# A chunked scan with two MLPs on one core: Silu by ScalarE in two blocks, and C B^T from rounded parts in the last twelve units

## The chip, the cores and the metric

One core of a Trainium2 chip runs the whole program. The metric is the device time of one execution in microseconds (us); lower is better. The core has five engines with a queue of instructions each, worked off in order: TensorE (PE, with its weight loads PEld), VectorE (DVE), ScalarE (ACT), GpSimd (POOL) and SyncE (SP, which here issues every DMA). A semaphore ties an instruction to what it needs on another engine.

## What is computed

The reference is a chain of three parts, all in float32:

```python
# 1: scan over 24 chunks of 32 steps, 4 batches x 8 heads, head_dim 32, state 16
M = einsum('bhin,bhjn->bhij', Cc, Bc) * L          # L = exp(cum_i - cum_j), lower triangle
y = M @ xc + (Cc @ state) * exp(cum)
state = exp(sum la) * state + Bx.sum
# 2: x = y as [3072, 256]
xn = x / sqrt(mean(x*x) + 1e-6) * rms_g
g = xn @ w_gate;  val = xn @ w_val                 # 256 -> 1536
x2 = (g * sigmoid(g) * val) @ w_out                # 1536 -> 256
# 3: h = x2 @ w_in (256 -> 1024); solu = h * softmax(h); layer norm over 1024, times g_ln
out = ln @ w_out2                                  # 1024 -> 256
```

## The kernel before, in words

The kernel uses chunks of 128 steps, not 32. A *unit* is 128 tokens of one batch with all 8 heads; there are 24 units (6 per batch, which carry a state from one to the next), in six *blocks* of 4 units, 512 tokens each.

**A unit's attention step.** `at_cb` (line 290) multiplies C by B^T for the eight heads, contraction over 16 rows, in float32: 8 matmuls, which the profile shows as 16 records. `at_mt` (L307, DVE) multiplies the result by the decay L, which ACT made with an exponential (`at_lexp`, L237; in the first four units `at_lpx`, L267). `at_y` (L321, L326, L331) makes the rows and the state's part; `at_ycb` issues the next unit's `at_cb` right behind it. Then follow a square (`at_sq`, L355, ACT), its column sum (`at_ms`, L361, PE), the root (L374, L379), its broadcast (L383), the copy and scale (`at_xc` L389, `at_xn` L394) and the split into a rounded part and a remainder (`at_xh` L401, `at_xl` L405).

**The split.** The large products run on operands that are rounded (fp32r), each as a rounded part and a remainder: high by high, low by high, high by low. So a 256-deep gate product of 512 tokens is 6 matmuls.

**The first MLP of a block** goes in 12 slices f of 128 of the 1536 features: gate (`pg`, L558), value (`pv`, L558), `th` = tanh(g/2) on ACT (L572), (th+1) g on DVE (`g_silu`, L576), times the value on DVE (`g_mul`, L580), rounding to `ah` (ACT, L586), remainder `al` (DVE, L592), and 2 x 3 matmuls into `po` (L600). `pg` and `pv` have one PSUM bank each, so the next gate product waits until the last one was read. The factor 2 that this form leaves is taken out at `x2_h` and `x2_l` (scale 0.5).

**The second MLP of a unit**: `ph` (L436, 12 matmuls), maximum, exponential, product on DVE and ACT, transposes `pt` (L514), split, `pf` (L538, 24 matmuls), output.

**Weights** arrive as raw 64-bit words. A piece (26 of them, 512 KB each) takes three DVE passes (`w_conv`: L116, L119, L122), a rounding on ACT (`w_hi`, L129) and a remainder on DVE or POOL (`w_lo`, L133). This work lies in the first 140 us, beside the start and the first blocks' MLP.

**The order** is written by a planner at build time. Each step is an `op` with an engine, an assumed duration, a due time, the steps it follows, the buffers it makes and uses. `plan` (in the same function) takes, again and again, the engine that can start first, and on it the step with the earliest due time among those that could start within a small slack; some DVE steps have an alternative on POOL (`alt`). Due times come from constants: `PRO` and `FIRST` (when block 0's MLP is due and how long it lasts), `Y0`, `YPOS` (attention steps), `EARLY`, `WGAP` (weights), `HLAG` (second MLP). What comes out is a fixed order on each engine.

Of the kernel before, what the change touches and what calls it, by code (L numbers as in the profile page):

```python
# [7 lines left out]
F32 = mybir.dt.float32  # L8
# [4 lines left out]
ALU = mybir.AluOpType  # L13
# [29 lines left out]
WGAP = 8.0  # L43
HLAG = (50.0, 26.0)
# [7 lines left out]
def fused_kernel(ctx, tc, aT, xbt, bcT, wg, wv, wo1, rg, wi2, wo2, gl, consts, out):  # L52
# [333 lines left out]
    def at_xc(u):  # L386
        d = st[u]
        d["xts"] = sp.tile([P, 2, P], F32, name="xts", bufs=BUFS["xts"])
        A.activation(d["xts"], d["y"][:, 0:256].rearrange("p (g i) -> p g i", g=2), AF.Copy)  # L389

    def at_xn(u):
        d = st[u]
        for g in range(2):
            V.scalar_tensor_tensor(out=d["xts"][:, g], in0=d["xts"][:, g], scalar=rgt[:, g:g + 1],  # L394
                                   in1=d["y"][:, 384:512], op0=ALU.mult, op1=ALU.mult)
# [293 lines left out]
    for u in range(NU):  # L689
# [7 lines left out]
        op(f"lbc{u}", "SP", 0.85, Y - 9, (ld_bc, u), new=[("bc", f"bc{u}")], kb=128)  # L697
# [32 lines left out]
        cbop = f"cb{u}" if u <= blk[0][1] else f"y{u-1}"  # L730
# [3 lines left out]
        yc = blk[0][1] <= u < NU - 1  # L734
# [17 lines left out]
        op(f"xc{u}", "ACT", 0.42, Y, (at_xc, u), after=[f"y{u}", f"sq{u}"], new=[("xts", f"xt{u}")], use=[f"y{u}", f"xt{u}"])  # L752
        op(f"xn{u}", "DVE", 0.6, Y, (at_xn, u), after=[f"rb{u}", f"xc{u}"], use=[f"y{u}", f"xt{u}"])
# [6 lines left out]
    for b in range(NB):  # L760
# [3 lines left out]
        for f in range(NF):  # L764
# [11 lines left out]
            op(f"si{s}", "DVE", v_us(N), t, (g_silu, b, f), after=[f"th{s}"], use=[f"th{s}", f"pg{s}"])  # L776
            op(f"mu{s}", "DVE", v_us(N), t, (g_mul, b, f), after=[f"si{s}", f"vm{s}"], use=[f"th{s}", f"pv{s}"])
# [123 lines left out]
    op("wd", "ACT", 0.35, 5.5, (c_wdec,), after=["sf"], use=["pd"])  # L901
    op("cst", "SP", 0.9, 5, (ld_cst,), kb=128)
    op("glt", "SP", 0.45, 40, (ld_glt,), kb=4)
    for u in range(2):
        ops[f"sbd{u}"]["after"].append("cst")
        ops[f"xn{u}"]["after"].append("cst")
# [3 lines left out]

    def plan():
        users = {}
        for o in ops.values():
            for key in set(o["use"]):
                users[key] = users.get(key, 0) + 1
# [25 lines left out]
        def est(o, e, margin=0.0):  # L941
            t = free[e]
            for a in o["after"]:
# [12 lines left out]
            if e == "SP" and len(dma_end) >= 8:  # L956
                t = max(t, dma_end[-8])
            return t

        while len(order) < len(ops):  # L960
            best = None
            dve = None
            for e, names in ready.items():
                if e == "POOL":
                    names = names + [nm for nm in ready["DVE"] if "alt" in ops[nm] and nm != dve]
                c = [(est(ops[nm], e, MARGIN.get(e, 0.0) if free[e] > PRO else 0.0), nm) for nm in names]
# [14 lines left out]
            if e != o["e"]:  # L981
                o = ops[nm] = dict(o, us=o["alt"][0], fn=o["alt"][1])
                ready["DVE"].remove(nm)
            else:
                ready[e].remove(nm)
            order.append((t, nm))
            if e == "SP":
                free[e] = t + o["us"]
                dma_free = max(dma_free, t + 1.3) + o["kb"] / 300.0
# [21 lines left out]
    with tc.manual_schedule():  # L1011
        S.dma_start(la, aT)
        S.dma_start(um, consts[:, 0:3 * P])
        S.dma_start(ident, consts[:, 3 * P:4 * P])
# [14 lines left out]
        V.tensor_scalar(out=nid, in0=ident, scalar1=-1.0, scalar2=None, op0=ALU.mult)  # L1029
# [70 lines left out]
```

## Time and profile before

| | us |
|---|---|
| median of 3 runs (565.73 to 566.2) | 565.83 |
| the profiled execution | 565.08 |
| its span, first to last instruction | 563.4 |
| PE busy | 546.5 (97%) |
| DVE busy | 390.9 (69%) |
| ACT busy | 290.3 (52%) |
| POOL busy | 84.8 (15%) |

The profiled execution is one of its own; its time lies 0.75 us under the median. "Busy" for PE means that at least one matmul was in flight; matmuls overlap, so a group's busy time is larger than what it adds to the path. The pitch from one start to the next is the better measure of cost. PEclk is the granted TensorE clock as a share of full speed; 0.50 is its lower level.

### The profile page before, as it was taken

Reading aid. Unit: us, or ns where it says so; the run is one execution under the profiler, and the core shown is the slowest. Engines: PE = TensorE matmul, PEld = TensorE weight load, DVE = VectorE, ACT = ScalarE, POOL = GpSimd, SP = SyncE. Lnnn points to the kernel's source line nnn. Section 1 sums busy time; section 2 is a strip of 40 time slices with the busy share of each in tenths; the row PEclk is TensorE's granted clock in tenths of the full one; section 3 lists DMA queues with packets and bytes.
Section 4 is the critical chain, followed back from the end, with each engine's and each line's share of the span. In section 5 each row is a group of like instructions: output and inputs, shape, how many; then the busy total and the mean of one; then the engine's idle time right before and its main releaser. Section 6 shows DMA issues by size and latency. Waiting matters only on the chain.

```text
span 563.4 us, 9443 instructions
## 1 busy us (share of the span) xinstructions
PE 546.5 (97%) x3544; PEld 461.1 (82%) x3544; DVE 390.9 (69%) x789; ACT 290.3 (52%) x654; POOL 84.8 (15%) x118
## 2 busy tenths in 40 slices
PE   9879998899999999999999999999999999999996
PEld 8757886687888888888888888888888888888795
DVE  5788999999876776575684574684674574564763
ACT  6437654666555564463474454554543353343464
POOL 2333323212221010110111100110100000000010
PEclk9579999999999999999999999999999999999999
DMA  7464765542022021121120220220200000000000
GB/s 213 132 212 140 216 203 194 182 145 71 14 72 76 2 80 47 43 72 36 54 76 11 75 70 10 80 70 10 72 2 9 10 1 9 11 1 10 9 20 30
DMA packets 44366, 39.33 MB, mean 70 GB/s; under 512 B 3936, under 2 KB 36896, under 8 KB 44320
## 3 DMA queue, kind: packets, MB, share of 16 engines
q1 hardware_dynamic: 44320, 38.72, 22.5%
q8 instruction: 28, 0.46, 0.4%
q14 instruction: 18, 0.15, 0.1%
HBM read 35.37 MB, written 3.34 MB: 69 GB/s over the span
## 4 chain that ended last, share of the span: by engine, by line
PE 81%; DVE 15%; DMA 2%; issue 1%; ACT 1%; SPq 0%; POOL 0%; DVEq 0%; ACTq 0%; POOLq 0%
PE pv L558 15%; PE pg L558 15%; PE po L600 14%; PE ph L436 12%; PE pf L538 12%; PE pt L514 4%; PE pcb L301 3%; DVE wt L119 2%; PE y L326 2%; DVE wt L122 2%; DVE th L580 2%; PE y L321 1%; DVE al L592 1%; DVE th L576 1%; DVE L L307 1%; DVE wt L116 1%
## 5 line engine op out<-in xcount | busy, mean ns | idle before, releaser
L586 ACT ACTIVATE ah<-th 128x512 fp32r<-128x512 f32 x72 | 45.2, 628 | 52.2 <-PE po L600 38.8
L580 DVE TENSOR_TENSOR th<-pv,th 128x512 f32<-128x512 f32 x72 | 49.8, 691 | 29.2 <-PE pv L558 24.1
L592 DVE TENSOR_TENSOR al<-th,ah 128x512 fp32r<-128x512 f32 x70 | 49.3, 704 | 26.0 <-ACT ah L586 25.6
L576 DVE SCALAR_TENSOR_TENSOR th<-th,pg 128x512 f32<-128x512 f32 x72 | 49.1, 682 | 20.0 <-ACT th L572 19.7
L558 PE MATMUL pg<-xh,wg_h 128*128 128x512 f32 x144 | 59.5, 413 | 2.3 <-ACT xh L401 1.2
L600 PE MATMUL po<-ah,wo_h 128*128 128x512 f32 x144 | 60.3, 419 | 0.0
L600 PE MATMUL po<-al,wo_h 128*128 128x512 f32 x144 | 56.7, 394 | 2.3 <-DVE al L592 2.3
L558 PE MATMUL pv<-xh,wv_h 128*128 128x512 f32 x144 | 58.4, 406 | 0.0
L558 PE MATMUL pg<-xh,wg_l 128*128 128x512 f32 x144 | 57.0, 396 | 0.0
L558 PE MATMUL pg<-xl,wg_h 128*128 128x512 f32 x144 | 56.8, 394 | 0.0
L600 PE MATMUL po<-ah,wo_l 128*128 128x512 f32 x144 | 56.7, 394 | 0.0
L558 PE MATMUL pv<-xl,wv_h 128*128 128x512 f32 x144 | 56.5, 392 | 0.0
L558 PE MATMUL pv<-xh,wv_l 128*128 128x512 f32 x144 | 56.4, 392 | 0.0
L572 ACT ACTIVATE th<-pg 128x512 f32<-128x512 f32 x72 | 42.6, 592 | 26.6 <-PE pg L558 26.4
L502 POOL TENSOR_TENSOR sc<-sc,mhalf 128x1 f32<-128x1 f32 x24 | 14.1, 587 | 263.6 <-DVE sc L497 263.6
L237 ACT ACTIVATE L<-L,cneg 128x128 f32<-128x128 f32 x160 | 50.5, 390 | 0.6 <-DMA L<-crow 0.6
L460 ACT ACTIVATE ut<-ph,sc 128x1024 f32<-128x1024 f32 x20 | 22.3, 1116 | 54.5 <-DVE sc L447 54.5
L538 PE MATMUL pf<-wo_h,uth 128*128 128x256 f32 x176 | 49.6, 282 | 0.3 <-DVE utl L528 0.2
L538 PE MATMUL pf<-wo_h,utl 128*128 128x256 f32 x176 | 49.6, 282 | 0.0
L538 PE MATMUL pf<-wo_l,uth 128*128 128x256 f32 x176 | 49.5, 281 | 0.0
L447 DVE TENSOR_REDUCE sc<-ph 128x1 f32<-128x1024 f32 x20 | 24.5, 1225 | 31.7 <-PE ph L436 31.7
L523 ACT ACTIVATE uth<-pt 128x512 fp32r<-128x512 f32 x44 | 26.0, 595 | 31.1 <-PE pt L514 30.9
(138 smaller groups left out, 1225.2 us busy)
## 6 DMA issues: line engine op xcount, KB each, us to landing
L<-crow SPq DMA_DIRECT2D x20, 512.0 KB
stage<-in_wo_dram SPq DMA_DIRECT2D x10, 512.0 KB
xb<-in_xbt_dram SPq DMA_DIRECT2D x24, 192.0 KB
stage<-in_wg_dram SPq DMA_DIRECT2D x6, 512.0 KB
bc<-in_bcT_dram SPq DMA_DIRECT2D x48, 64.0 KB
stage<-in_wv_dram SPq DMA_DIRECT2D x6, 512.0 KB
out_dram<-ob SPq DMA_DIRECT2D x24, 128.0 KB
stage<-in_wi_dram SPq DMA_DIRECT2D x4, 512.0 KB
```

Source lines behind the costliest of these rows:

```text
L237: A.activation(d["L"][:, h], d["L"][:, h], AF.Exp, bias=cneg[:, u * 8 + h:u * 8 + h + 1])
L436: T.matmul(ph[c], xx[:, kk, k * P:(k + 1) * P], ww[:, kk, 512 * c:512 * c + 512], start=(i == 0), stop=(i == 5))
L447: V.tensor_reduce(out=sc[:, 0:1], in_=ph[0], axis=AX.X, op=ALU.max, negate=True)
L523: A.activation(d["uT"][0][:, 4 * c:4 * c + 4].rearrange("p k t -> p (k t)"), d["ptc", c], AF.Copy)
L538: T.matmul(d["pf"][:, 0:DM], uu[:, k], ww[:, k], start=(k == 0 and i == 0), stop=(k == 7 and i == 2))
L558: T.matmul(ps[:, :n], ww[:, kk, f * P:(f + 1) * P], xx[:, kk, :n], start=(i == 0), stop=(i == 5))
L572: A.activation(d["th"], d["pg"], AF.Tanh, scale=0.5)
L576: V.scalar_tensor_tensor(out=d["th"], in0=d["th"], scalar=1.0, in1=d["pg"], op0=ALU.add, op1=ALU.mult)
L580: V.tensor_tensor(out=d["th"], in0=d["pv"], in1=d["th"], op=ALU.mult)
L586: A.activation(d["ah"], d["th"], AF.Copy)
L592: e.tensor_tensor(out=d["al"], in0=d["th"], in1=d["ah"].bitcast(F32), op=ALU.subtract)
L600: T.matmul(po[b, m][:, :n], ww[:, f, m * P:(m + 1) * P], aa, start=(f == 0 and i == 0), stop=(f == NF - 1 and i == 2))
```

## The change

1. In blocks 0 and 1 ACT computes Silu(g) itself; the DVE step `g_silu` is gone there and the product becomes (2 silu) times value. Silu lies in another activation table than the exponential, so the built program has more table loads on ACT.
2. For units 12 to 23, B and C come by one DMA into 128 rows: the same 32 rows four times (512 KB written instead of 128). ACT rounds both (`at_hi`); DVE or POOL puts the remainder of B into the lower 64 rows (`at_blo`), DVE the remainder of C by a mask in rows of odd slots (`at_clo`); two masked copies separate the two heads that share 32 rows (`at_c0` on ACT, `at_c1` on DVE). One matmul of 128 rows and 256 columns then adds all four products of parts for two heads: 4 matmuls a unit. They are a step of their own and no longer tied to `at_y`.
3. The row scale `rms_g` moves from DVE (`at_xn`, two passes, now one) to ACT (`at_xc`, one pass, now two).
4. Where the planner sees PE idle for over 0.5 us during the start, it puts in small matmuls on unused columns (`warm`); five stand in the program. The identity's load is a planned step, and its negative is no longer made.
5. Constants of the planner change, and it counts 1.3 us for a change of table.

```diff
-FIRST = 63.0
+FIRST = 70.0
-Y0 = (9.0, 4.0)
-YPOS, YSPAN = 0.65, 1.0
+Y0 = (10.0, 3.0)
+YPOS, YSPAN = 0.3, 1.0
-SLACK = 0.1
-SLACK0 = 0.1
+SLACK = 0.2
+SLACK0 = 0.3
-EARLY = (-1.0, 1.5, 4.0, 6.0)
+EARLY = (-5.0, -1.0, 4.0, 6.0)
-WGAP = 8.0
-HLAG = (50.0, 26.0)
+WGAP = 6.0
+WOFF = -10.0
+HLAG = (70.0, 26.0, 3)
+SILU = 2
+TABLE = 1.3
...
+    SPLIT = blk[0][1] + blk[1][1] + blk[2][1]
+
+    def ld_bc4(u):
+        d = st.setdefault(u, {})
+        d["bc"] = sp.tile([P, 8, P], F32, name="bc")
+        S.dma_start(d["bc"], bcT[u].unsqueeze(0).to_broadcast([4, 32, 1024]))
+
+    def at_hi(u):
+        d = st[u]
+        d["bh"], d["ch"] = (sp.tile([P, 4, P], F32R, name=nm, tag="wt", bufs=BUFS["wt"]) for nm in ("bh", "ch"))
+        A.activation(d["bh"], d["bc"][:, 0:4], AF.Copy)
+        A.activation(d["ch"], d["bc"][:, 4:8], AF.Copy)
+
+    def at_blo(u, e):
...
+        e.tensor_tensor(out=bh[64:128], in0=bc[64:128, 0:4], in1=bh[64:128].bitcast(F32), op=ALU.subtract)
+
+    def at_clo(u):
...
+        V.scalar_tensor_tensor(out=bc[:, 4:8], in0=ch.bitcast(F32), scalar=nc_mask, in1=bc[:, 4:8],
+                               op0=ALU.mult, op1=ALU.add)
+
+    def at_c0(u):
...
+        A.activation(d["cb"][:, :, 0], d["bc"][:, 4:8], AF.Copy, scale=h0_mask)
+
+    def at_c1(u):
...
+        V.tensor_scalar(out=d["cb"][:, :, 1], in0=d["bc"][:, 4:8], scalar1=h1_mask, scalar2=1.0,
+                        op0=ALU.mult, op1=ALU.mult)
+
+    def at_cbr(u):
+        d = st[u]
+        d["pcb"] = pp.tile([P, 8, P], F32, name="pcb", tag="hc")
+        for q in range(4):
+            T.matmul(d["pcb"][:, 2 * q:2 * q + 2].rearrange("p h i -> p (h i)"), d["bh"][:, q],
+                     d["cb"][:, q].rearrange("p h i -> p (h i)"), start=True, stop=True)
...
-        A.activation(d["xts"], d["y"][:, 0:256].rearrange("p (g i) -> p g i", g=2), AF.Copy)
+        for g in range(2):
+            A.activation(d["xts"][:, g], d["y"][:, g * P:(g + 1) * P], AF.Copy, scale=rgt[:, g:g + 1])
...
+        V.tensor_tensor(out=d["xts"], in0=d["xts"], in1=d["y"][:, 384:512].unsqueeze(1).to_broadcast([P, 2, P]), op=ALU.mult)
...
-        A.activation(d["th"], d["pg"], AF.Tanh, scale=0.5)
+        if b < SILU:
+            A.activation(d["th"], d["pg"], AF.Silu)
...
-        V.tensor_tensor(out=d["th"], in0=d["pv"], in1=d["th"], op=ALU.mult)
+        if b < SILU:
+            V.scalar_tensor_tensor(out=d["th"], in0=d["th"], scalar=2.0, in1=d["pv"], op0=ALU.mult, op1=ALU.mult)
...
+            op(f"lbc{u}", "SP", 0.45, Y - 14, (ld_bc4, u), new=[("bc", f"bc{u}")], kb=1300)
...
+            T.matmul(st[u]["y"][:, 322:384], ones, ones[:, 0:62], start=True, stop=True, skip_group_check=True)
```

Three places in the built order. **ACT during the start**, where units 0 and 1 are worked on (`sq` is the square of the rows, `wv_h`, `wg_h` roundings of weights, `L` exponentials of the next units). Before:

```order
L267 ACTIVATE L<-pg,cneg 128x128 x4
L267 ACTIVATE L<-pv,cneg 128x128 x4
L129 ACTIVATE wv_h<-wt 128x2x256
L355 ACTIVATE sq<-y 128x256
L389 ACTIVATE xts<-y 128x256
L267 ACTIVATE L<-pg,cneg 128x128 x4
```

Now:

```order
L274 ACTIVATE L<-pg,cneg 128x128 x4
L274 ACTIVATE L<-pv,cneg 128x128 x4
L408 ACTIVATE sq<-y 128x256
L443 ACTIVATE xts<-y,rgt 128x128 x2
L136 ACTIVATE wg_h<-wt 128x2x256
L274 ACTIVATE L<-pg,cneg 128x128 x4
```

The square of unit 0 had the rounding of the second weight piece ahead of it and now follows the exponentials at once; the first weight piece is rounded behind it.

**ACT in block 0, from the second to the third Silu** (`th<-pg`; `ah` is the rounding of its product, `e` a small exponential). Before:

```order
L572 ACTIVATE th<-pg 128x512
L237 ACTIVATE L<-L,cneg 128x128 x8
L246 ACTIVATE e_515<-e_515 128x128
L586 ACTIVATE ah<-th 128x512
L572 ACTIVATE th<-pg 128x512
```

Now:

```order
L625 ACTIVATE th<-pg 128x512
L244 ACT_TABLE_LOAD
L244 ACTIVATE L<-L,cneg 128x128 x8
L253 ACTIVATE e_504<-e_504 128x128
L644 ACTIVATE ah<-th 128x512
L244 ACTIVATE L<-L,cneg 128x128 x8
L136 ACTIVATE wo_h<-wt 128x512
L136 ACTIVATE wg_h<-wt 128x2x256
L253 ACTIVATE e_517<-e_517 128x128
L625 ACT_TABLE_LOAD
L625 ACTIVATE th<-pg 128x512
```

Two table loads stand between the two passes, and two units' exponentials are worked off between them instead of one. From the first to the last Silu of the two blocks there are 18 loads, in the whole program 22; before there were 2, both ahead of the first gate product.

**PE at C B^T of unit 13.** Before:

```order
L558 MATMUL pg<-xh,wg_l 128x512
L326 MATMUL y<-L,xb 32x128 x8
L331 MATMUL y<-xb 32x64 x4
L301 MATMUL pcb<-bc 128x128 x8
L514 MATMUL pt<-ident,ut 128x128 x4
```

Now:

```order
L658 MATMUL po_1385<-ah,wo_h 128x512
L658 MATMUL po_1385<-al,wo_h 128x512
L658 MATMUL po_1385<-ah,wo_l 128x512
L359 MATMUL pcb<-cb,bh 128x256 x4
L610 MATMUL pg<-xh,wg_h 128x512
```

The eight matmuls behind the unit's rows are gone; four stand by themselves between products of the MLP, well ahead of the next unit's rows.

## Rows read from the trace of the kernel before

**Rows 1.** The page: span, PE's busy time, and PE's slices with its clock

```profile
span 563.4 us, 9443 instructions
PE 546.5 (97%) x3544; PEld 461.1 (82%) x3544; DVE 390.9 (69%) x789; ACT 290.3 (52%) x654; POOL 84.8 (15%) x118
...
PE   9879998899999999999999999999999999999996
...
PEclk9579999999999999999999999999999999999999
```

**Rows 2.** Busy time by stage (from:to, length, engines, clock, DMA share, GB/s)

```profile
16.64:28.42 11.78, 11.78 (x77) 10.87 (x78) 8.44 (x21) 4.61 (x15) 4.92 (x7) 0.50 0.39 125
...
40.22:43.90 3.68, 3.68 (x9) 2.83 (x10) 3.29 (x8) 1.32 (x3) 0.00 (x0) 0.50 1.10 339
...
core 0: us, PE busy (x) PEld busy (x) DVE busy (x) ACT busy (x) POOL busy (x), PEclk, DMA share, GB/s
40.22:140.00 99.78, 95.39 (x613) 75.78 (x614) 96.36 (x179) 61.26 (x151) 27.73 (x31) 0.98 0.54 170
140.00:450.00 310.00, 310.00 (x2040) 262.88 (x2039) 202.11 (x407) 157.59 (x352) 38.44 (x56) 1.00 0.15 45
520.00:563.40 43.40, 38.03 (x253) 33.74 (x251) 24.73 (x68) 22.18 (x47) 2.75 (x5) 0.99 0.06 19
```

**Rows 3.** Timeline of ACT and PE in the start (start, length, [idle before, what ended it])

```profile
15.16 0.63 ACT L129 ACTIVATE wv_h<-wt 128x512 fp32r<-128x512 f32 x1 [2.00 <-DVE wt L122]
15.69 0.37 ACT L355 ACTIVATE sq<-y 128x256 f32<-128x256 f32 x1
...
16.64 1.01 PE L361 MATMUL y<-ones,sq 128*128 128x1 f32 x4 [1.95 <-DVE s L340]
...
38.53 0.48 PE L383 MATMUL y<-ident,r 128*128 128x128 f32 x1 [2.32 <-POOL r L379]
40.22 0.79 PE L558 MATMUL pg<-xh,wg_h 128*128 128x512 f32 x1 [1.21 <-ACT xh L401]
```

**Rows 4.** Chain that ended last, pieces in order of time (start, length, what)

```profile
52.21 1.09 PE pcb L301 x16
...
72.46 0.60 DVE al L592
...
161.31 2.83 PE pf L538 x24
...
174.89 1.39 PE pg L558 x6
...
278.87 2.77 PE ph L436 x12
...
300.55 2.77 PE ph L436 x12
```

**Rows 5.** Timeline of ACT in block 0: pitch from start to start

```profile
50.68 0.62 ACT L129 ACTIVATE wv_h<-wt 128x512 fp32r<-128x512 f32 x1
51.20 2.44 ACT L237 ACTIVATE L<-L,cneg 128x128 f32<-128x128 f32 x8
53.54 0.62 ACT L586 ACTIVATE ah<-th 128x512 fp32r<-128x512 f32 x1
```

**Rows 6.** Costliest groups: the old Silu step on DVE

```profile
L576 DVE SCALAR_TENSOR_TENSOR th<-th,pg 128x512 f32<-128x512 f32 x72 | 49.1, 682 | 20.0 <-ACT th L572 19.7
```

**Rows 7.** Timeline of PE, 92 to 139 us: its waits for DVE

```profile
95.75 0.50 PE L600 MATMUL po<-al,wo_h 128*128 128x512 f32 x1 [1.84 <-DVE al L592]
...
106.72 0.50 PE L600 MATMUL po<-al,wo_h 128*128 128x512 f32 x1 [0.49 <-DVE al L592]
...
111.87 0.50 PE L558 MATMUL pg<-xh,wg_h 128*128 128x512 f32 x1 [0.98 <-DVE th L576]
```

**Rows 8.** Timeline of ACT: the table load before the first exponential

```profile
5.53 1.28 ACT L267 ACT_TABLE_LOAD   x1 [2.06 <-DVE cneg L1026]
6.83 1.14 ACT L267 ACTIVATE L<-pg,cneg 128x128 f32<-128x128 f32 x4
```

More of the change, by code (lines that the diff above doesn't have):

```diff
@@ L653, in wdue @@
             return gdue(0, 2 * c + (LAG if q == 2 else 0)) - 4.0
-        return start[1] - 4.0 + (i - 18) * WGAP
+        return start[1] + WOFF + (i - 18) * WGAP
     for i in range(26):
@@ L729, in fused_kernel @@
                use=[f"bc{u}", f"pcb{u}"] + ([f"pcb{u}'"] if cbt(u) else []))
[L730 removed]
+        cbop = f"cb{u}" if u <= blk[0][1] or u >= SPLIT else f"y{u-1}"
+        if u >= SPLIT:
+            op(f"cb{u}", "PE", 0.5, Y - 12.0, (at_cbr, u), after=cbok + Lok[1], new=[("hc", f"pcb{u}")],
+               use=[f"bh{u}", f"cb{u}", f"pcb{u}"])
         for hp in range(2):
             op(f"mt{u}.{hp}", "DVE", 0.7, Y - 1, (at_mt, u, hp), after=[cbop] + Lok[hp], use=[f"pcb{u}'" if hp and cbt(u) else f"pcb{u}", f"L{u}"])
[L734 removed]
+        yc = blk[0][1] <= u < NU - 1 and u + 1 < SPLIT
         op(f"y{u}", "PE", (1.4 if not s0 else 1.1) + (1.05 if yc else 0.0), Y, (at_ycb if yc else at_y, u),
@@ L751, in fused_kernel @@
         op(f"rb{u}", "PE", 0.12, Y, (at_rb, u), after=[f"pw{u}"], use=[f"y{u}"])
-        op(f"xc{u}", "ACT", 0.42, Y, (at_xc, u), after=[f"y{u}", f"sq{u}"], new=[("xts", f"xt{u}")], use=[f"y{u}", f"xt{u}"])
-        op(f"xn{u}", "DVE", 0.6, Y, (at_xn, u), after=[f"rb{u}", f"xc{u}"], use=[f"y{u}", f"xt{u}"])
+        op(f"xc{u}", "ACT", 0.6, Y, (at_xc, u), after=[f"y{u}", f"sq{u}"], new=[("xts", f"xt{u}")], use=[f"y{u}", f"xt{u}"])
+        op(f"xn{u}", "DVE", 0.42, Y, (at_xn, u), after=[f"rb{u}", f"xc{u}"], use=[f"y{u}", f"xt{u}"])
         op(f"xh{u}", "ACT", 0.42, Y, (at_xh, u), after=[f"xn{u}"] + ([f"xh{u-1}"] if k else []), new=[("xs", f"xs{b}")] if k == 0 else [],
@@ L901, in fused_kernel, with ld_ident, c_nid @@
     op("wd", "ACT", 0.35, 5.5, (c_wdec,), after=["sf"], use=["pd"])
+    def ld_ident():
+        S.dma_start(ident, consts[:, 3 * P:4 * P])
+    def c_nid():
+        V.tensor_scalar(out=nid, in0=ident, scalar1=-1.0, scalar2=None, op0=ALU.mult)
+    op("idn", "SP", 0.45, 4, (ld_ident,), kb=64)
+    if VIA_PE:
+        op("nid", "DVE", 0.25, 6, (c_nid,), after=["idn"])
+        for i in VIA_PE:
+            ops[f"wp{i}"]["after"].append("nid")
+    ops["rb0"]["after"].append("idn")
     op("cst", "SP", 0.9, 5, (ld_cst,), kb=128)
@@ L905, in fused_kernel, with warm @@
         ops[f"sbd{u}"]["after"].append("cst")
-        ops[f"xn{u}"]["after"].append("cst")
+        ops[f"xc{u}"]["after"].append("cst")
     early = [f"lpe{u}.{g}" for u in range(NPE) for g in range(2)] + ["e1p"] + ["cr0", "cr1"]
     ops["wh22"]["after"] += early + ["sf"]
+    def warm(u, n):
+        if u not in st:
+            return
+        for _ in range(n):
+            T.matmul(st[u]["y"][:, 322:384], ones, ones[:, 0:62], start=True, stop=True, skip_group_check=True)
+    for nm, o in ops.items():
+        if o["e"] == "ACT" and nm[:2] in ("lx", "e1", "ex", "wd"):
+            o["tab"] = "exp"
     def plan():
         users = {}
+        table = ["exp"]
         for o in ops.values():
@@ L942, in est @@
             t = free[e]
+            if e == "ACT" and o.get("tab", table[0]) != table[0]:
+                t += TABLE
             for a in o["after"]:
@@ L958, in est, with mg @@
             return t
-        while len(order) < len(ops):
+        def mg(nm, e):
+            if nm[0] == "w" and nm[1] != "d":
+                return WMG
+            return MARGIN.get(e, 0.0) if free[e] > PRO else 0.0
+        lasty = None
+        while len(end) < len(ops):
             best = None
@@ L965, in plan @@
                     names = names + [nm for nm in ready["DVE"] if "alt" in ops[nm] and nm != dve]
-                c = [(est(ops[nm], e, MARGIN.get(e, 0.0) if free[e] > PRO else 0.0), nm) for nm in names]
+                c = [(est(ops[nm], e, mg(nm, e)), nm) for nm in names]
                 c = [x for x in c if x[0] < INF]
@@ L985, in plan @@
                 ready[e].remove(nm)
+            if nm[0] == "y":
+                lasty = int(nm[1:])
+            if e == "PE" and lasty is not None and t < PRO + 6 and t - free[e] > 0.5:
+                order.append((free[e], (warm, lasty, int((t - free[e]) * FILL / 0.22))))
             order.append((t, nm))
+            if e == "ACT":
+                table[0] = o.get("tab", table[0])
             if e == "SP":
                 free[e] = t + o["us"]
-                dma_free = max(dma_free, t + 1.3) + o["kb"] / 300.0
+                dma_free = max(dma_free, t + 1.3) + o["kb"] / DRATE
                 end[nm] = dma_free + 1.0
```

48 lines of the change are left out of this document (38 added, 10 removed).

## The prediction, made before the change had run

> **What bounds the kernel now.** I read the page's engine table and slices first, then the busy time by stage, then PE's own waits, and only then the chain. PE is busy 546.5 of 563.4 us, and the slices say where it is not: at the start, a little in slices 6 to 10, and at the very end [rows 1]. By stage: from 140 to 450 us PE is busy without a gap at clock 1.00, so there only PE's work counts [rows 2]. From 40.22 to 140 us (block 0's MLP and most of block 1's, beside the conversion of the weights) DVE is busy 96.36 of 99.78 us, and yet PE is idle for only 99.78 - 95.39 = 4.39 us [rows 2]. Many links of the chain there are DVE's, so one might expect a lot from freeing DVE; the idle time says that 4.4 us is all that PE can get back in that stage. The start is the weak place: the first gate product begins at 40.22 [rows 3]. At 16.64 PE had waited 1.95 us; from 16.64 to 28.42 it is busy all 11.78 us at clock 0.50, the lower of its two levels (1.2 instead of 2.4 GHz), so about 5.9 us of that is lost; it waits 2.32 and 1.21 us more before 40.22, and the first 3.68 us of block 0 run at 0.50 again [rows 2, 3].
>
> **The sum is made against the profiled execution**, 565.08 us (span 563.4); the median of the runs is 0.75 above it, which I add at the end. Many numbers of the planner change too, so nearly every queue is reordered; I cost the stages, not each move.
>
> **C B^T of the last 12 units: -7.4.** Before: 8 matmuls (16 records) with 16 rows, 1.09 us of the chain [rows 4]. Now 4 matmuls with 128 rows and 256 columns on rounded operands. The nearest row is pf: same rows, same columns, same kind, 24 in 2.83 us, so 0.118 each and 0.47 for four [rows 4]. 12 x (1.09 - 0.47) = 7.4, in a stage where PE has no gap, so all of it counts. The other end: each costs as much as a 512-column product, 2.77 / 12 = 0.23 [rows 4], then 0.92 for four and the gain is 2.0. I take 7.4, since pf has the very shape.
>
> What pays for it: ACT makes three more 128x512 passes a unit (rounded B, rounded C, masked C) at a pitch of 0.52 (50.68 to 51.20) [rows 5], 1.6 us. DVE makes two or three (the remainders of B, seven times on DVE and five on POOL, and of C, and the other mask) at up to 0.60 [rows 4], 1.8 us at most. A unit's turn lasts 300.55 - 278.87 = 21.7 us there [rows 4]; DVE is busy 202.11 / 310 = 65% and ACT 157.59 / 310 = 51% [rows 2]; with 1.8 and 1.6 us more in a turn of 21.1 they go to about 75% and 60%. PE's lead covers that, unless a queue in fixed order holds a step that PE wants soon. I put **+1**, with 0 and +4 (0.33 a unit) as ends. The load of B and C grows from 128 to 512 KB a unit; DMA is busy 0.15 there [rows 2]: nothing. That load's buffer is now freed by the masked copies and not by PE, and the loads behind it on SP wait with it; it is issued 14 us ahead instead of 9, so nothing again.
>
> **Silu on ScalarE in blocks 0 and 1 and the new order there: -2.** DVE loses 24 passes [rows 6]; 23 lie between the first and the last product of gate and value of the two blocks, 23 x 0.60 = 13.8 us of queue [rows 4]. By the two orders some 6 us comes into that stretch from elsewhere (five more remainders of weights that POOL or the start had, three more conversion passes, steps of the first two new C B^T), less three remainders of a that POOL takes. So DVE's content there falls by about 8 us, while PE's own stays: the two blocks' first gate product begins at 40.22 and their last at 174.89 [rows 3, 4], 134.7 us, of which 4.4 are idle, 1.8 slow clock and some 3 the changes between kinds of matmul, so 125 of work. The multiplication by 2 rides in the product's pass and the row norm is one pass instead of two. The most this can return is PE's 4.39 us, which contains waits of 1.84 and 0.49 for the remainders of a and 0.98 for the old Silu step [rows 7]. The Silu pass also no longer holds the bank of the gate product.
>
> Against it stands ACT: the new order has 20 more table loads. 18 of them lie between the first and the last Silu, at 1.28 us each [rows 8], so 23.1 us. With a few more steps (three more weight roundings, the norm's copy in two, the row masks of the first two new C B^T, one more unit's exponentials at 2.34 for eight [rows 5]), some 33 us come in; ACT was busy 61.26 of 99.78 us [rows 2], 61%, which is 77 us of those 125. So 110 of 125: it fits, but ACT is no longer slack. Ends: -4.4 (every wait goes) and +8 (waits in fixed order); I take -2, nearer to the gain since contents decide most.
>
> **The start: -5.** In the old order ACT stood 2.00 us in front of a weight rounding, with the square that PE's next sum needed behind it, and PE waited 1.95; then came the slow stretch [rows 3]. In the new order the square stands first. DVE has 65 instructions (25.1 us at their pitches) ahead of the last remainder of block 0's rows, now 50 (19.9): six conversion passes and a few small steps have left the front. If PE's gap stays short and the clock stays at 1.00, the 5.9 us of the slow stretch come back and perhaps 3 us of waits, so -9; if PE still runs at 0.50 there, about 0, since then it is PE's own pace that sets the start. I take -5. The five small matmuls that PE now does while it waits lie in idle time: 0. The 1.84 us lost at 0.50 from 40.22 on I leave as it is, for PE's last waits before it stay (square, norm, rounding).
>
> **The tail: 0.** From 520 us on PE is busy 38.03 of 43.4 us [rows 2]; the last units' steps are reordered, by as much as 1.5 either way.
>
> Sum: -7.4 + 1 - 2 - 5 = -13.4; 565.08 - 13.4 = 551.7, and with 0.75 the median is **552.4 us**. With the ends of all terms: between 544 and 563.
>
> **Rivals.** A difference of about 0.2% (1.1 us) is what this kernel's runs can tell from none.
>
> *A. Only C B^T pays.* The start stays at PE's half clock and what DVE gives back ACT's table loads take: -7.4 + 1 to 3, so 559 to 563 with the median's offset (558 to 564.7 as a case). For it: the slow stretch had PE busy all the time, so a short gap is no proof that the clock holds. Against: DVE has 5 us less ahead of the start. 0.18.
>
> *B. ACT becomes the bound in blocks 0 and 1 (slower).* The place: ACT's queue, where a table load stands before an exponential pass and another before the next Silu, and PE's next gate product waits for the bank that this Silu frees. The price of a switch is seen only after 2.06 us of idleness (load 1.28, next pass 0.02 later) [rows 8]; behind a running pass it may cost more, from 1.28 up to, say, twice the load, 2.57. At 2.57 ACT's content is 110 + 18 x 1.29 = 133 us against PE's 125, so +8 with perfect interleaving, and up to +25 if ACT also keeps some 17 us in which it waits for gates. With the -7.4 + 1 - 5 of the rest that is 562 to 579. Content alone binds from 15 / 18 = 0.8 us above the load; slower than before it gets when a switch costs about 1 to 1.5 us above its load. 0.10. The Trainium skill speaks for this rival: "ScalarE: Activation LUTs", section "What ACT_TABLE_LOAD costs", gives 1283 ns for the load, which the trace confirms, and 1380 ns more for a drain, which no row here shows; by its 2.66 us a switch (an estimate from that page) the 18 switches would add 24.8 us to ACT's content and case B would be the outcome.
>
> *C. Everything pays.* The clock holds, all waits of PE between 40 and 140 us go: -7.4 - 9 - 4.4 = -20.8, 545. 0.10 for 547 and less.
>
> *D. No effect that can be told*: B in a mild form against C B^T. 0.03.
>
> **How the numbers follow.** The forecast (547 to 558) gets 0.59, A 0.18, B 0.10, C 0.10, D 0.03. The range takes the forecast, most of A and most of C: 544 to 563. Faster than 564.7: 0.59 + 0.18 + 0.10 = 0.87; within 0.2%: 0.03; slower than 567.0: 0.10.
>
> **What would show it.** Right: the four new matmuls take about 0.47 us a unit on the chain; the stretch from 140 to 450 us is still without a gap; the first gate product begins between 33 and 37 us, and the clock's row in 16 to 28 us is above 0.5; ACT's busy time rises by some 25 us for the loads and 19 for the new passes, DVE's stays about level. Wrong: pf's rate is not met by the new matmuls; PE waits for Silu or table loads in blocks 0 and 1 for more than some 5 us; the first gate product is at 40 again; PE shows gaps at the transposes of the later units because the new DVE passes stand before the softmax steps.

## The result and the profile after

The changed kernel takes 569.77 us (median of 7 executions, 567.25 to 570.66), the kernel before on the same chip 565.15 (median of 7). The ratio is 1.0102, 95% interval 1.0075 to 1.0129: **slower by 1%**, outside the predicted range. The profiled execution took 569.77, so its span can be set beside that of before.

The page of the changed kernel: span, PE, its slices and clock, the DMA queue that carries the loads (packets, MB, share of 16 engines) and the chain by engine.

```profile
span 568.1 us, 9215 instructions
...
PE 545.0 (96%) x3410; PEld 456.1 (80%) x3410; DVE 389.1 (68%) x758; ACT 342.5 (60%) x734; POOL 102.2 (18%) x136
...
PE   9979999999999999999989999999999999999896
...
PEclk9959989989999999999989999999999999999999
...
q1 hardware_dynamic: 45136, 43.44, 26.1%
...
PE 65%; DVE 13%; ACT 12%; DMA 7%; issue 2%; SPq 1%; POOL 0%; ACTq 0%; DVEq 0%; POOLq 0%
```

Against [rows 1], PE now has an 8 and a clock of 8 in slice 21 (284 to 298 us), where before there was no gap, and the clock's row shows two more 8s and a 5 in the first nine slices, where there was a 5 and a 7. DMA is 7% of the chain and ACT 12%; on the page of before they are 2% and 1%:

```profile
PE 81%; DVE 15%; DMA 2%; issue 1%; ACT 1%; SPq 0%; POOL 0%; DVEq 0%; ACTq 0%; POOLq 0%
```

Busy time by stage (from:to, length, engines, clock, DMA share, GB/s):

```profile
16.64:28.42 11.78, 10.49 (x133) 8.89 (x135) 9.68 (x23) 7.05 (x24) 7.38 (x11) 0.92 0.68 201
28.42:36.13 7.71, 4.59 (x40) 3.92 (x32) 3.85 (x10) 2.09 (x6) 1.18 (x2) 0.50 0.69 204
36.13:40.22 4.09, 4.09 (x10) 3.15 (x11) 3.76 (x7) 2.34 (x4) 0.00 (x0) 0.50 0.91 277
36.13:140.00 103.87, 99.06 (x611) 78.17 (x612) 90.98 (x162) 77.17 (x161) 26.62 (x26) 0.95 0.49 155
140.00:450.00 310.00, 305.22 (x1890) 256.54 (x1889) 210.41 (x408) 194.51 (x420) 56.16 (x76) 0.99 0.22 62
520.00:568.10 48.10, 40.49 (x265) 35.67 (x263) 27.57 (x73) 24.02 (x51) 3.29 (x6) 1.00 0.05 17
```

Set beside [rows 2]: the first gate product begins at 36.13 instead of 40.22, a gain of 4.1. From 140 to 450 us PE was without a gap; now it is idle for 310 - 305.22 = 4.78 us, and the clock falls to 0.99. At the end the idle time has gone from 5.37 to 7.61 us. I also went through PE's timeline from the first gate product on and took from each distance between two starts the usual pitch of what stands there. Lost time by that account, before and after: up to 60 us 2.4 and 3.2; from 60 to 160 us 7.2 and 10.7; **from 160 to 520 us 2.6 and 11.8**; behind that 3.1 and 5.3. That is 15.7 more. Minus 4.1 of the start and 7.4 of C B^T it leaves 4.2, and the spans differ by 4.7.

What stands behind the 11.8 is seen around 280 us. The chain of the changed kernel there (start, length, what):

```profile
277.48 9.20 DMA L<-crow
...
286.70 0.44 ACT L L244 x2
...
287.30 0.68 ACT L L244 x2
287.98 0.49 ACT uth L575
...
288.49 0.70 DVE utl L580
...
289.24 4.63 PE pf L590 x24
```

PE stood 2.23 us in front of this `pf`, and its first sixteen matmuls, from 289.24 to 292.68, have a pitch of 0.215 us against the usual 0.118, so that all 24 take 4.63 us instead of 2.83. The rounding `uth` that it needs has nothing to do with L. It stands behind L's exponentials in ACT's queue, and these wait for a load that takes 9.20 us. In the kernel before the same 512 KB, issued at 173.28, were 4.08 us later in use by an exponential that had waited for them (timelines of SP and of ACT):

```profile
173.28 0.40 SPq L227 DMA_DIRECT2D L<-crow  x1
```

```profile
177.36 2.46 ACT L237 ACTIVATE L<-L,cneg 128x128 f32<-128x128 f32 x8 [0.44 <-DMA L<-crow]
```

All such waits of the changed kernel, by engine and releaser (us in total, times, longest):

```profile
ACT L L244 <- DMA L<-crow: 11.6, 6, 3.0
DVE xb L238 <- DMA xb<-in_xbt_dram: 6.3, 4, 2.6
```

Before, ACT waited 0.6 us for L and DVE not at all for `xb`. What is ahead of L in the queue shows in the timeline of SP and in the busy time by stretches of 2 us:

```profile
202.75 0.56 SPq L326 DMA_DIRECT2D bc<-in_bcT_dram  x1
206.27 0.37 SPq L234 DMA_DIRECT2D L<-crow  x1
```

```profile
204.00:206.00 2.00, 2.00 (x26) 1.66 (x28) 0.89 (x3) 1.06 (x2) 0.00 (x0) 1.00 0.26 80
206.00:208.00 2.00, 2.00 (x30) 1.91 (x23) 1.54 (x4) 1.01 (x3) 0.00 (x0) 1.00 0.25 81
208.00:210.00 2.00, 2.00 (x17) 1.90 (x16) 0.16 (x1) 0.47 (x1) 0.19 (x1) 1.00 0.90 236
```

While the new load of B and C runs alone, the DMA engines are busy to 0.25, as much as four of sixteen, and move 80 GB/s; from 204.2 to 207.9 us the trace has four packets of 4 KB under way at nearly every moment. Its shape in the diff is `[4, 32, 1024]`. So the theory to test: one broadcast DMA with an outer size of 4 keeps four engines busy for long, the part of L that falls to these four comes behind it, and ACT's fixed order carries the delay to PE. The middle step can be seen in the trace, which marks sixteen landings for one load of L. For the load issued at 277.48 twelve of them come 4.6 to 5.3 us after the issue, and the last four 8.7 to 9.2 us after it: the slow load's own last four come at 284.86 to 285.40, and L's behind them at 286.14 to 286.68. Between the twelve and the last four the share is back at 0.25:

```profile
283.00:285.00 2.00, 2.00 (x12) 1.64 (x11) 2.00 (x4) 0.68 (x2) 0.00 (x0) 1.00 0.25 76
```

In all six places where L was issued less than 5 us behind the slow load, its last four landings come 1.2 to 5.1 us after the twelfth; in the kernel before, all sixteen of each load from 150 us on have landed within 4.2 us. The rivals: the table loads of Silu, the new passes on ACT and DVE, or the new order as such.

### The profile page after: what moved, and what is told of

It reads as the page before. It is cut to its first block, busy times and chain, and to the rows that moved or that the text cites. A ratio compares the mean times of both kernels' runs of the same rounds, so it can differ in the third digit from the quotient of the medians.

```text
span 568.1 us, 9215 instructions
## 1 busy us (share of the span) xinstructions
PE 545.0 (96%) x3410; PEld 456.1 (80%) x3410; DVE 389.1 (68%) x758; ACT 342.5 (60%) x734; POOL 102.2 (18%) x136
## 4 chain that ended last, share of the span: by engine, by line
PE 65%; DVE 13%; ACT 12%; DMA 7%; issue 2%; SPq 1%; POOL 0%; ACTq 0%; DVEq 0%; POOLq 0%
PE pv L610 13%; PE pg L610 13%; PE po L658 12%; PE pf L590 9%; PE ph L488 8%; DMA L<-crow 5%; ACT L L244 3%; PE pt L566 3%; PE y L379 2%; ACT jk L540 1%; DVE ut L522 1%; DVE utl L580 1%; DVE sc L499 1%; DMA xb<-in_xbt_dram 1%; PE y L374 1%
## 5 line engine op out<-in xcount | busy, mean ns | idle before, releaser
L650 DVE TENSOR_TENSOR al<-th,ah 128x512 fp32r<-128x512 f32 x63 | 44.3, 702 | 33.9 <-ACT ah L644 33.8
L610 PE MATMUL pg<-xh,wg_h 128*128 128x512 f32 x144 | 60.8, 423 | 3.4 <-ACT xh L453 1.7
L244 ACT ACTIVATE L<-L,cneg 128x128 f32<-128x128 f32 x160 | 50.4, 390 | 11.8 <-DMA L<-crow 11.6
L631 DVE SCALAR_TENSOR_TENSOR th<-th,pg 128x512 f32<-128x512 f32 x48 | 32.8, 683 | 12.6 <-ACT th L627 12.1
L638 DVE TENSOR_TENSOR th<-pv,th 128x512 f32<-128x512 f32 x48 | 33.1, 690 | 8.4 <-PE pv L610 5.2
L488 PE MATMUL ph<-wi_h,xh 128*128 128x512 f32 x96 | 38.1, 397 | 0.0
L590 PEld LDWEIGHTS pf<-wo_h,uth 128*128 128x128 f32 x176 | 33.8, 192 | 4.9 <-DVE utl L580 4.0
```

The lines of the kernel that those rows point to most:

```text
L244: A.activation(d["L"][:, h], d["L"][:, h], AF.Exp, bias=cneg[:, u * 8 + h:u * 8 + h + 1])
L488: T.matmul(ph[c], xx[:, kk, k * P:(k + 1) * P], ww[:, kk, 512 * c:512 * c + 512], start=(i == 0), stop=(i == 5))
L590: T.matmul(d["pf"][:, 0:DM], uu[:, k], ww[:, k], start=(k == 0 and i == 0), stop=(k == 7 and i == 2))
L610: T.matmul(ps[:, :n], ww[:, kk, f * P:(f + 1) * P], xx[:, kk, :n], start=(i == 0), stop=(i == 5))
L631: V.scalar_tensor_tensor(out=d["th"], in0=d["th"], scalar=1.0, in1=d["pg"], op0=ALU.add, op1=ALU.mult)
L650: e.tensor_tensor(out=d["al"], in0=d["th"], in1=d["ah"].bitcast(F32), op=ALU.subtract)
```

## The experiments

Every comparison is with the kernel before on the same chip. Its medians were between 563.1 and 563.7 us there, so I compare ratios where differences are small.

**1. The form of the DMA alone.** Nothing else moves.

```diff
-        S.dma_start(d["bc"], bcT[u].unsqueeze(0).to_broadcast([4, 32, 1024]))
+        for s in range(4):
+            S.dma_start(d["bc"][32 * s:32 * s + 32], bcT[u])
```

> The 512 KB load of B and C by one broadcast DMA ([4, 32, 1024]) is replaced by four DMAs of [32, 1024], into the same places; the order of everything else is that of the changed kernel. Theory (the slow broadcast load is what costs: in the trace of the changed kernel the DMA engines are busy to a share of 0.25 for 8 to 10 us behind each of its issues, and the load of L behind it takes 9.2 us): the share rises well over 0.25 behind these issues, ScalarE's waits for L (11.6 us in 6 waits) fall under 3 us, and most of the 10.8 us that TensorE loses in 160 to 400 us comes back, so about 561 to 564 us. Rival 1 (the extra passes on ScalarE and VectorE stand in the way of others): 568 to 571 us, although the waits for L go. Rival 2 (the transfer is limited by its bytes or by its destination, not by the form of the DMA): the share stays at 0.25 and the time within 1 us of 569.8.

Measured: 559.52 us, ratio 0.9935 (0.9912 to 0.9958), against 1.0102: some 10 us come back (9.4 by the ratios), a little more than the theory said. The kernel now beats the one before. Its waits for L, its stage from 140 to 450 us and two stretches behind the issue (the four DMAs at 201.06, L at 204.57):

```profile
ACT L L244 <- DMA L<-crow: 0.7, 1, 0.7
```

```profile
140.00:450.00 310.00, 309.63 (x1922) 261.31 (x1922) 213.95 (x412) 196.38 (x421) 55.79 (x75) 1.00 0.21 62
```

```profile
203.00:205.00 2.00, 2.00 (x34) 1.70 (x33) 1.16 (x2) 0.94 (x2) 0.00 (x0) 1.00 0.61 178
205.00:207.00 2.00, 2.00 (x19) 2.00 (x18) 0.91 (x3) 0.71 (x3) 0.00 (x0) 1.00 0.68 207
```

The share is 0.61 and more, the waits of ACT for L are gone, and PE has its gapless middle back, with the new passes all in place (ACT 196.38, DVE 213.95 in this stage). So these passes are not the cause; nor are the bytes, which are the same.

**2. Its place in the queue.** The old form, kept back until the next load of L has been issued (or until the rounding that needs it).

```diff
     def ld_bc4(u):
+        pend.append(u)
+
+    def ld_pend():
...
         S.dma_start(d["L"], r.unsqueeze(0).to_broadcast([P, 8, P]))
+        ld_pend()
...
     def at_hi(u):
+        ld_pend()
```

> The changed kernel with its broadcast load of B and C in the old form ([4, 32, 1024]), but issued behind the next load of L instead of ahead of it. Theory (place in the queue, not the slow load itself): ScalarE's waits for L fall from 11.6 to under 3 us and 559 to 563 us comes out, like the run with four DMAs. Rival (B and C themselves come too late at 80 GB/s): the waits move to the rounding passes on ScalarE that read bc, and the time is 565 us or more.

Measured: 583.14 us, ratio 1.0354 (1.0315 to 1.0393). The first half of the theory held, ACT's waits for L fell to 1.4 us. But what now stood behind the slow load waited in its place:

```profile
DVE xb L241 <- DMA xb<-in_xbt_dram: 18.4, 5, 6.6
```

and `bh` itself once for 8.1 us. The time is in the rival's range, though the wait for B and C themselves is the smaller part. A miss as a cure: in both places that were tried, some load stands behind it.

**3. The same kind of load in the kernel before**, into a tile that nobody reads, first at the end of each group of loads, then ahead of L.

```diff
             S.dma_start(bc[64 * hp:64 * hp + NS], bcT[u][NS * hp:NS * hp + NS, :])
+        if u >= 12:
+            dz = sp.tile([P, 4, P], F32, name="dz", bufs=1)
+            S.dma_start(dz, bcT[u][:, 0:512].unsqueeze(0).to_broadcast([4, 32, 512]))
```

> The kernel before, with a second load of B and C behind the first one in units 12 to 23: half the columns, to 4 x 32 rows by one broadcast DMA of [4, 32, 512] (256 KB), into a tile that nobody reads. Nothing else moves. Theory: the share of the DMA engines is 0.25 behind these issues for about 3 to 4 us (half of what the changed kernel's load takes), the loads behind it come later by that, and as L is issued with little to spare the kernel gets slower by 0.5 to 4 us. Rival (a slow load that nobody waits for is hidden, since the transfers of L were early enough): within 0.5 us of 565.

Measured: 563.11 us, ratio 0.9990 (0.9968 to 1.0011). No cost: the next load of L comes 15 us or more behind it, and ACT has no new wait. In the second the same three lines stand in `ld_L`, ahead of L's own load:

> The kernel before with the same unread 256 KB broadcast load as in the run before it, but issued ahead of the load of L of units 12 to 23 instead of at the end of each group of loads. Theory (the slow broadcast load costs only through the loads that stand behind it in the queue): L lands about 3 us later, ScalarE waits for L (0 us with the load at the end), and the time is 2 to 6 us above 563.1. Rival (L had that much to spare in the kernel before, and it is the changed kernel's later issue of L that makes it short): within 1 us of 563.1.

Measured: 563.53 us, ratio 0.9998 (0.9974 to 1.0022). No cost either, but by SP's timeline the test did not do what it should. L waits on SP for its buffer, and the unread load in front of it had gone 8 to 15 us earlier in all units but one. In that one it went 1.1 us before L, and only there did ACT wait for L (0.78 us).

**4. The same, where it must hold L up**: L's first head goes first, so that the buffer's wait is over, then the unread load, then the other seven heads.

```diff
-        S.dma_start(d["L"], r.unsqueeze(0).to_broadcast([P, 8, P]))
+        n = 1 if u >= 12 else 8
+        S.dma_start(d["L"][:, 0:n], r[0:n].unsqueeze(0).to_broadcast([P, n, P]))
+        if u >= 12:
...
+            S.dma_start(d["L"][:, 1:8], r[1:8].unsqueeze(0).to_broadcast([P, 7, P]))
```

> The kernel before with the unread 256 KB broadcast load of [4, 32, 512] placed where it must hold L up: the load of L of units 12 to 23 is split, its first head (64 KB) goes first, then the unread load, then the other seven heads, all at the time at which L was issued (in the run with the load ahead of L it had gone 8 to 10 us before L in all units but one, since L waits for its buffer, and was over by then). Theory: the heads behind it land 3 us later, ScalarE waits 1 to 3 us in each of some 10 units, and the time is 1 to 6 us above 563.6. Rival (ScalarE has that much to spare in the kernel before, where it is busy for 52% of the span): waits appear on ScalarE, the time stays within 1 us.

Measured: 568.52 us, ratio 1.0100 (1.0065 to 1.0135): 5 us, from a load that nobody reads. And with the same bytes to the same places by four DMAs:

```diff
-            S.dma_start(dz, bcT[u][:, 0:512].unsqueeze(0).to_broadcast([4, 32, 512]))
+            for s in range(4):
+                S.dma_start(dz[32 * s:32 * s + 32], bcT[u][:, 0:512])
```

> As the run with the unread 256 KB load between the first head of L and the rest, but by four DMAs of [32, 512] instead of one broadcast DMA of [4, 32, 512]: the same bytes to the same places at the same point of the queue. Theory (the form decides: one broadcast DMA of outer size 4 keeps a quarter of the DMA engines busy): the waits for L (36.5 us in 13 with the broadcast form) fall by more than half and the time is 563 to 566 us against 568.5. Rival (256 KB more ahead of L cost that much in any form): 567.5 to 569.5 us.

Measured: 563.51 us, ratio 1.0004 (0.9979 to 1.0028). ACT's waits for L in the two, broadcast and four DMAs:

```profile
ACT L L242 <- DMA L<-crow: 36.5, 13, 4.7
```

```profile
ACT L L243 <- DMA L<-crow: 11.4, 9, 2.4
```

So the form decides, not the bytes. ACT's waits are 2.8 us on average in the first and 1.3 in the second: in this order the one costs 5 us and the other nothing that can be told.

**5. Table loads.** Tanh in place of Silu in the changed kernel, and in that with four DMAs.

```diff
-            A.activation(d["th"], d["pg"], AF.Silu)
+            A.activation(d["th"], d["pg"], AF.Tanh)
```

Blocks 0 and 1 then leave Silu out and use tanh(g), so these two kernels don't compute the reference; they only show what the loads cost.

> Silu is replaced by Tanh in blocks 0 and 1, with one factor and one order of instructions as in the changed kernel, so that the 22 table loads fall to one or two; these two blocks then use tanh(g) in place of Silu(g). Theory (the slow load of B and C is the main cause, the table loads cost little, since ScalarE has spare time): TensorE's losses in 160 to 400 us stay, those in 60 to 120 us (10.7 us) fall by 1 to 3 us, so 567 to 569.5 us. Rival (ScalarE is the bound of blocks 0 and 1 through 22 loads of 1.28 us): most of the 10.7 us comes back there, 560 to 564 us.

Measured: 567.45 us, ratio 1.0060 (1.0035 to 1.0085).

> Both edits: four DMAs for the load of B and C, and Tanh in place of Silu in blocks 0 and 1 (which then use tanh(g)). If the two costs lie in different stretches, as the theory says, the gains add: 559 to 563 us, below both single edits by about the other one's gain. If one shared cause (ScalarE being late) stands behind both, the gain of both together is less than the sum by 2 us or more.

Measured: 557.25 us, ratio 0.9881 (0.9861 to 0.9900). Without the 20 table loads 2.4 us are gained in the one, 2.3 in the other, each known to about 2 us; so far as that goes the two costs add. It is more in the clock than in waits. The changed kernel and the same with Tanh, from 60 to 80 and from 100 to 120 us:

```profile
60.00:80.00 20.00, 18.97 (x104) 15.18 (x103) 18.86 (x35) 13.31 (x28) 2.69 (x3) 0.91 0.61 194
100.00:120.00 20.00, 17.84 (x107) 13.91 (x106) 16.53 (x34) 13.87 (x31) 6.29 (x6) 0.91 0.61 198
```

```profile
60.00:80.00 20.00, 19.38 (x111) 14.93 (x110) 19.80 (x37) 11.78 (x29) 2.48 (x3) 1.00 0.58 190
100.00:120.00 20.00, 19.44 (x121) 15.63 (x120) 19.54 (x37) 13.12 (x29) 9.25 (x9) 1.00 0.67 207
```

**6. No Silu, four DMAs**, in two orders: as the planner makes it, and with the planner told of the four DMAs.

```diff
-SILU = 2
+SILU = 0
...
-            op(f"lbc{u}", "SP", 0.45, Y - 14, (ld_bc4, u), new=[("bc", f"bc{u}")], kb=1300)
+            op(f"lbc{u}", "SP", 1.7, Y - 14, (ld_bc4, u), new=[("bc", f"bc{u}")], kb=512)
```

> The changed kernel with four DMAs for the load of B and C and with no Silu (the number of blocks that use it set to 0): Tanh and a second VectorE pass in all blocks, no table loads, and an order that the planner makes for it. Theory (Silu saves a VectorE pass per step but its 22 table loads cost about as much): within 3 us of the run with four DMAs, 557 to 563 us. Rival (VectorE is what blocks 0 and 1 wait for, and the saved pass is worth more than the loads): 563 us or more.

Measured (the first part of the diff): 563.73 us, ratio 1.0014 (0.9992 to 1.0036), just outside the theory's range and in the rival's.

> The same with the planner told that the load of B and C takes 1.7 us of the queue and 512 KB: what is computed, and how, is that of the run beside it, and only the order differs. If the order alone is worth several us, as the two runs with four DMAs and Silu (559.5 and 566.4 us) say, this one lies 3 us or more from the run beside it, on either side; if the load and Silu were all, within 1.5 us of it.

Measured (both parts): 565.04 us, ratio 1.0027 (1.0005 to 1.0050), within 1.5 us of the run beside it, so here the planner's numbers for the load are worth little. The second part alone, with Silu:

> Four DMAs for the load of B and C, and the planner told so (1.7 us of the issuing queue and 512 KB, in place of 0.45 us and 1300 KB): it then places the loads, and with them everything, anew. Theory (the order of the run with four DMAs was made for a load of 1300 KB, and hardly any wait for L is left in it): 556 to 561 us. Rival (the planner's order was already as good as it gets, and a new one brings other waits): 560 to 564 us.

Measured: 566.37 us, ratio 1.0058 (1.0034 to 1.0081), 6.9 us longer than with the planner's old numbers, though the operations are the same. Most of it is one wait: PE stands 4.2 us for a Silu between 140 and 160 us. A better model of one load gave a worse order. In the run without Silu DVE is busy 97.52 of 104 us from 36 to 140 us and PE waits 4.6 us for `g_silu`: so in that order DVE is a bound, which Silu on ACT takes away. What Silu alone is worth isn't isolated, since this order is another than that of experiment 1.

**7. The new C B^T with the old constants**: four DMAs, no Silu and the planner's constants of the kernel before; then the same order with the one broadcast DMA. The move of the row scale to ACT and the planned load of the identity are still in both, so C B^T isn't quite alone. The main constants:

```diff
-FIRST = 70.0
+FIRST = 63.0
...
-YPOS, YSPAN = 0.3, 1.0
+YPOS, YSPAN = 0.65, 1.0
...
-SLACK = 0.2
-SLACK0 = 0.3
+SLACK = 0.1
+SLACK0 = 0.1
...
-HLAG = (70.0, 26.0, 3)
+HLAG = (50.0, 26.0, 1)
...
-SILU = 2
+SILU = 0
```

> The new C B^T alone: the changed kernel with the old planner's constants, no Silu and four DMAs for the load of B and C, so that start and blocks 0 and 1 are planned as before and units 12 to 23 have the new C B^T. Theory: TensorE's work falls by 7.4 us, and with 1 to 3 us for the new passes 557 to 561 us. Rival (the planner's order around the new operations gives the gain back): 563 us or more.

Measured: 559.02 us, ratio 0.9927 (0.9905 to 0.9949), as fast as with the start's and Silu's changes [experiment 1]. But its first gate product, too, begins earlier than the 40.22 of the kernel before:

```profile
37.62 0.79 PE L611 MATMUL pg<-xh,wg_h 128*128 128x512 f32 x1 [1.02 <-ACT xh L454]
```

So part of its gain can be the start's (the gate product begins 2.6 us earlier in this trace and 1.9 in that of the next run, whose order is the same).

> The kernel with the new C B^T alone (559.0 us), with its load of B and C as the one broadcast DMA of [4, 32, 1024] again; order and all else as there. Theory (the slow load holds up the loads behind it, whatever the order): ScalarE's and VectorE's waits for L, xb and e return, and the time is 4 to 12 us longer, 563 to 571 us. Rival (it was the changed kernel's order that made the load hurt): within 2 us of 559.

Measured: 600.40 us, ratio 1.0668 (1.0632 to 1.0704): 41 us for the form of one DMA in 12 units, more than either theory allowed. Its chain around 280 us, its stage from 140 to 450 us and PE's largest wait:

```profile
275.54 9.84 DMA L<-crow
...
285.40 0.03 ACT L L244
...
285.71 0.97 ACT L L244 x3
286.68 0.49 ACT uth L575
...
287.19 0.70 DVE utl L580
...
287.94 5.33 PE pf L590 x24
```

```profile
140.00:450.00 310.00, 284.87 (x1707) 240.31 (x1706) 197.46 (x387) 168.71 (x380) 46.63 (x57) 0.95 0.21 59
```

```profile
PE pf L590 <- DVE utl L580: 24.7, 8, 4.9
```

It is the chain of the changed kernel link by link, now in seven of the twelve units. Its `pf` after the wait takes 5.33 us for 24, where 2.83 was usual [rows 4]: the wait is paid again in the clock, 0.95 on average from 140 to 450 us where four DMAs had 1.00. After each of the six longest waits (3.2 to 4.9 us) sixteen `pf` take 2.7 to 3.6 us instead of 1.9. From the first exponential behind each issue of L, in those units where the load of B and C was issued less than 5 us ahead of it:

| kernel | issues | L in use after | ACT's wait for it |
|---|---|---|---|
| changed, one DMA | 6 | 6.83 to 12.62 | 0.58 to 3.02 in 5 |
| experiment 7, one DMA | 7 | 7.16 to 9.86 | 1.37 to 5.81 in 7 |
| experiment 7, four DMAs | 7 | 3.92 to 5.70 | 1.15 in 1 |

**8. The old C B^T in all units**, all else as in the change.

```diff
-    SPLIT = blk[0][1] + blk[1][1] + blk[2][1]
+    SPLIT = NU
```

> The changed kernel with the old C B^T in all 24 units (the limit from which the new form applies set to 24), so that what is left is Silu in blocks 0 and 1 and the new order; the planner makes an order of its own for it. Theory: the matmuls of C B^T hold their old 7.4 us on TensorE, the slow loads are gone, the start keeps its gain of 4 us and blocks 0 and 1 lose about 3 us more than before: 564 to 567 us, against 559.5 us with the new C B^T and four DMAs. Rival (the new C B^T saves next to nothing once its passes are paid): 559 to 561 us.

Measured: 576.06 us, ratio 1.0223 (1.0190 to 1.0256). Inconclusive for C B^T: the order made for it loses 5.4 us between 360 and 380 us alone, by the account of PE's timeline. It does say that the rest of the change, in an order of its own, is no gain.

## Why the prediction was wrong

**The step that failed** is "The load of B and C grows from 128 to 512 KB a unit; DMA is busy 0.15 there [rows 2]: nothing", with "it is issued 14 us ahead instead of 9, so nothing again". Both halves were wrong, and the cost is some 10 us (experiment 1: 559.52 against 569.77, or 9.4 us by the ratios). Without it the ratio of experiment 1 puts the kernel at 561.5 beside the 565.15 of before, inside the predicted range.

- A mean share of 0.15 over 310 us tells nothing of one transfer. The load runs on a quarter of the engines (0.25, 80 GB/s), so 512 KB take 6 us and more. The leading 4 in `[4, 32, 1024]` stood in the diff. The Trainium skill, "DMA: Bandwidth & Descriptors", section "Rules for kernel authors", states that an outermost dimension of size c below 16, such as a leading broadcast of c copies, confines a DMA to at most c engines; the share of 0.25 agrees, and the rule, not weighed in the prediction, spoke against this change.
- 14 us ahead is the planner's due time, not the issue. SP waited 62.4 us in 6 times for the masked copies that free the buffer, and in six units the load went out only 0.6 to 4.3 us ahead of L. The prediction saw that "the loads behind it on SP wait with it" and then took the lead for granted. The short lead by itself is harmless: with four DMAs SP waits as long for these copies (59.3 us in 6), and nothing is late.

**+1 for what pays for C B^T (0 to +4)** was the right place with a wrong price. "A queue in fixed order holds a step that PE wants soon" is what happens, on ACT, through L, not through the new passes. These cost little: with four DMAs PE is idle for 0.37 us from 140 to 450 us, where the slow load had made it 4.78.

**C B^T, -7.4**: right within a tenth for PE's own time. The four matmuls, start to start, take 0.46 to 0.56 us in eleven of the twelve units of the changed kernel (0.79 in one, with a wait), 0.49 on average; 0.47 was predicted, and 1.09 it was before [rows 4]. So 12 x 0.60 is 7.2. Net of its passes it was to give 6.4; experiment 7 gained 0.73% (0.51 to 0.95), 4.1 us, and part of that can be the start's, so the net gain of C B^T isn't isolated.

**The start, -5**: -4.1, and -5.1 in the trace of experiment 1, whose order is the same (its first gate product begins at 35.08). The clock was 0.92 instead of 0.50 from 16.64 to 28.42 us [rows 2], but then fell to 0.50 up to 40 us. So the prediction's "the clock stays at 1.00" came nearly true, for one stretch only: in the next PE stood idle for 3.12 of 7.71 us, and at the first gate product the clock was at 0.50, as before.

**Blocks 0 and 1, -2**: a loss of about 3.5 by the account of PE's timeline. PE's idle time hardly moved (4.39 before, 4.81 after), but behind its waits the clock fell (0.98 before, 0.95 after). With Tanh the stretch from 60 to 160 us loses some 3.5 us less by such an account, in both kernels of experiment 5; so what is lost here goes with the table loads. Contents predicted that ACT's queue would fit, and it fits; the prediction did not see that single steps stand late behind a table load. One such place ends with a wait of 1.19 us of PE for Silu, after this piece of the chain:

```profile
108.44 2.45 ACT L L244 x8
110.90 0.52 ACT wi_h L136
111.42 0.96 ACT xh L667 x2
...
112.59 1.28 ACT L625
...
113.89 0.60 ACT th L625
...
114.54 2.26 PE pg L610 x6
```

The table loads cost 2.3 to 2.4 us in all (experiment 5), so rival B named a real cost and far too high a one. The drain behind its price does not show: the 20 loads behind a running pass start 0.01 to 0.02 us after it ends, and in all but one of these places the next pass starts 0.01 us after the load.

```profile
42.52 0.60 ACT L625 ACTIVATE th<-pg 128x512 f32<-128x512 f32 x1
43.14 1.28 ACT L244 ACT_TABLE_LOAD   x1
44.43 1.87 ACT L244 ACTIVATE L<-L,cneg 128x128 f32<-128x128 f32 x6
```

The trace here differs from the 1380 ns that the Trainium skill, "ScalarE: Activation LUTs", section "What ACT_TABLE_LOAD costs", adds to its 1283 ns; the measurement decides.

**The tail, 0 (1.5 either way)**: +2.2, from 5.37 to 7.61 us of idle time. It is 7.51 with four DMAs and 4.78 with the old planner's constants, so it goes with the new constants.

With the slow load's cost taken off, the sum was still short: it forecast a gain of 13.4 us, and experiment 1 gained 3.7 (2.4 to 5.0, by its ratio). Of the 9.7 us between them about 5.5 are the blocks', 2 the tail's and 1 the start's; the rest is within the interval. Terms of this size were beyond an argument from contents, since orders differ by as much: the planner's number for one load moved the time by 6.9 us. How the planner's constants act on single steps was not followed further, and why the order without the new C B^T is so slow stays open.

**The range.** "With the ends of all terms: between 544 and 563" holds for the lower end only. The bad ends of the terms (-2 for C B^T, +4 for its passes, +8 for the blocks, 0 for the start, +1.5 for the tail) add up to 577.3, above the measured time; the upper end of 563 was narrower than the working behind it. In rival A, -7.4 + 1 to 3 makes 559.4 to 561.4 and not 559 to 563.

The fastest that compute the reference are the changed kernel with four DMAs (559.52) and that of experiment 7 with four DMAs (559.02); they can't be told apart.

## What to carry to other kernels

Read the shape of a new DMA before its size: one whose outer dimension is 4 ran on a quarter of the engines, and four DMAs of 32 rows cured it. A load that nobody waits for can still cost, through what is issued behind it, so look at SP's timeline for what is issued while it still runs (the delays here came with 0.6 to 5.4 us between the issues, and none showed from 7 us on), and on the receiving engine for what stands behind the wait. And a due time in a planner is no lead: what frees the buffer sets the issue.

## What was not expected of the hardware

- The price of a slow load depends on its place in the order. The same 512 KB cost some 10 us in 12 units in the changed kernel and 41 us (3.4 a unit) in the order of experiment 7; 256 KB cost nothing with L 15 us behind, and 5 us right ahead of L.
- A wait of PE can cost more than its length. In experiment 7 with the slow load, 24.7 us of waits for `utl` go with a loss of 41 us; behind one wait of the chain shown, 24 `pf` took 2.5 us longer than usual.
- 20 more table loads of 1.28 us cost 2.3 to 2.4 us of the whole, where ACT is busy for 60% of the span.
